# A third W' buffer, loads at set steps, low words on GpSimd and new priorities in a planned attention-and-FFN kernel

## Chip, cores and metric

The kernel runs on one core of one Trainium2 chip. The metric is the time of one execution on the device in microseconds (us). The core has five engines that matter here: TensorE (PE in the profile, with its weight loads as PEld), VectorE (DVE), ScalarE (ACT), GpSimd (POOL) and SyncE (SP), which starts all the DMA transfers. Each of them works through its own instructions in the order in which the program holds them.

## The reference

Eight batches of eight heads, 576 rows of 64 numbers each. Thirty-two packed queries per head first attend over keys and values; then every query attends over the 32 packed results. A feed-forward layer with GELU follows, whose weights arrive as 64-bit floats.

```python
def sm_attn(qq, kk, vv):
    s = scale * np.matmul(qq, kk.transpose(0, 1, 3, 2))
    a = np.exp(s - np.max(s, axis=-1, keepdims=True))
    a = a / (np.sum(a, axis=-1, keepdims=True) + 1e-09)
    return np.matmul(a, vv)
p_packed = sm_attn(p, k, v)            # 8 x 8 x 32 x 64
x = sm_attn(q, p_packed, p_packed)     # then as 4608 x 512
h = x @ w_in                           # 512 x 2048
g = 0.5 * h * (1.0 + erf(h * inv_sqrt2))
out = g @ w_out                        # 2048 x 512
```

## The kernel before

**Tiling.** Batches go in four pairs (NP), the 2048 hidden units in four blocks of 512 (NF), so there are 16 units u (NU), each with eight steps: j is the batch of the pair, c one of four groups of 128 hidden units. A step n is a *hidden product* (h, L1184: twelve products of a three-part split, or L1175 in unit 0, plain 32-bit), a GELU on ScalarE (L1206), a split of its result into two words (L1213 on ScalarE, L1215 on VectorE, GpSimd for the rest of the rows in L1226 and L1227) and an *output product* (o, three times four products in L1236 to L1238), with one more set for the edge rows in each unit (o_edge).

**W'.** The second attention's product with the packed results and the first layer are folded: W' = packed results times w_in (`packed_w_in`, L1118, tile wps). It runs on the array in 64x32 tiles, where the others use it whole. ScalarE rounds it (L1129) and VectorE takes the rest (L1134). One buffer for each j, `wps[0]` and `wps[1]`, holds the result; it comes free with the last hidden product of its j. Both its PSUM tile and those of hidden products and of most scores come from `wide`, which has two.

**Weights.** They are decoded from 64-bit to two 32-bit words: ScalarE takes the absolute value of the high word (L1052) and scales the low word (L1053), VectorE repairs the exponent (L1060, L1061) and puts the sign in (L1066), GpSimd adds (L1080, L1088) and, for w_out, subtracts (L1094). The first pass stores them (`ws`); pairs 1 to 3 read them back (w<-ws, L1017).

**Attention.** For each chunk of four heads: transposes of keys and queries, key scores (L657), exponential (L739), transposes of it (L761, L764) and their copies (L771, L774), packed products (L799), query scores, centring (L878), exponential (L884), scaling (L898). In pair 0, keys and queries are loaded in rows of whole heads (L553) and transposed by TensorE with copies by ScalarE or VectorE (L592, L596); `FIRST` says which engine does what. In later pairs they are loaded in four blocks for each half (L563) and transposed by VectorE (L581). A pair's attention runs beside the hidden and output products of the pair ahead of it.

**Order.** All of it is written out while the program is built. Each piece of work is a task; it yields an `Op` with an engine and an assumed duration, or an `Event` that it waits for. `Order` plays the tasks through once to find how long the chain behind each is, corrects that by the tables SLACK, EARLY and SOONER, and plays them again: a free engine takes the ready Op of the highest priority whose buffers are free (`issue`), and its instructions are written in that order. So the tables set every engine's order, SyncE's too. On the chip an engine waits at an instruction whose input is late, and all behind it wait too. Before the first output product, a free TensorE gets a dummy product (L1157). `LATER["from"]` says at which step of the block ahead a pair's work may begin (`pair_started`); all its loads may then go.

A tile whose buffer was first lent to a dummy carries the name "idle" in the profile; only L1157 is a dummy.

Of the kernel before, what the change touches and what calls it, by code (L numbers as in the profile page):

```python
# [19 lines left out]
P = 128  # L20
# [26 lines left out]
MODE_SWITCH = 0.1  # L47
# [5 lines left out]
    "batch0": 1.805,  # L53
    "batch1": 2.067,
    "attention": 2.371,
    "load0": 0.169,
    "load": 0.137,
    "w_in0": 3.068,
    "w_out0": 1.984,
    "w_in": 0.766,  # L60
    "w_out": 1.189,
    "packed_w_in": 1.103,
# [3 lines left out]
    "batch0": 14.5,  # L66
    "batch1": -9.1,
    "attention": -0.5,
    "load0": -0.0,
    "load": 9.1,  # L70
    "w_in0": 3.4,
    "w_out0": 7.3,
    "w_in": -0.4,
    "w_out": -4.9,
    "packed_w_in": -4.5,
    "steps": -3.6,
# [3 lines left out]
    "0_0_0": 13.7,  # L80
    "0_0_1": 16.8,
    "0_1_0": -11.6,
    "0_1_1": -4.7,
    "0_2_0": -3.1,
    "0_3_0": -1.5,
    "0_4_0": -28.2,
    "0_5_0": -0.7,
    "chunk_0_0": -19.0,
    "chunk_0_1": 89.8,
    "chunk_1_0": -3.5,  # L90
    "chunk_1_1": -5.4,
    "softmax1": 48.6,
    "softmax1_0_0": 40.2,
    "softmax1_0_1": 36.3,
    "softmax1_1_0": -5.1,
    "softmax1_1_1": -10.6,
    "softmax2": -48.0,
    "softmax2_0_0": -26.1,
    "softmax2_0_1": -48.7,
    "softmax2_1_0": -69.0,  # L100
    "softmax2_1_1": -47.5,
    "wp_0_0": -28.4,
    "wp_0_1": 17.6,
    "wp_1_0": -21.6,
    "wp_1_1": -51.8,
# [21 lines left out]
    "from": (2, 0, 0, 0),  # L127
# [33 lines left out]
    "turn": {"k": ('ACT', 'ACT', 'ACT', 'ACT'), "q": ('ACT', 'DVE', 'ACT', 'ACT')},  # L161
# [21 lines left out]
class Ring:  # L183
# [7 lines left out]
    def has_room(self, name, before=0):  # L191

        if self.order.dry:
            return True
        n = len(self.held) + before
        if self.names and self.names[n] != name:
            return False
        return n < self.bufs or self.held[n - self.bufs] is None
# [64 lines left out]
class Order:  # L263
# [105 lines left out]

    def issue(self, engine):  # L370
        ready = self.ready[engine]
        for i, (_, _, op, go_on, begin) in enumerate(ready):
            if not op.takes or all(r.has_room(name, n if r is op.takes[0][0] else 0) for n, (r, name) in enumerate(op.takes)):
                del ready[i]
                break
# [55 lines left out]
def packed_attention_gelu_ffn(ctx: ExitStack, tc: tile.TileContext, q, k, v, p, w_in, w_out, out):  # L431
# [27 lines left out]
    def plan(order):  # L459
# [5 lines left out]

        def small(i, b):
# [18 lines left out]
        wraws = ring("wraw", 2, [P, FB, 2], I32)  # L485
# [3 lines left out]
        wps = [ring(f"wp{j}", 1, [P, 2, 2, FB], F32R) for j in range(2)]  # L489
# [9 lines left out]
        wps[0].names = ["q_0_1"] + [f"wp_{u}_0" for u in range(NU)]  # L499
        wps[1].names = ["v_0_1"] + [f"wp_{u}_1" for u in range(NU)]  # L500
# [20 lines left out]
        a2_used, plain_a2_ready = ([Event(n) for _ in range(2)] for n in (1, 2))  # L521
        pair_started = [Event() for _ in range(NP + 1)]
        scored = [Event(4) for _ in range(NP)]
        a2T, plain_a2, pp = {}, {}, {}
# [24 lines left out]

        def load(bt, name, src, c, step):  # L550
# [14 lines left out]
            cost, fn = ((1, 590e3), rows) if bt.b < 2 else ((4, 1640e3, 2), blocks)  # L565
# [41 lines left out]
        def load_values(s, step):  # L607
            heads = slice(4 * s.hh, 4 * s.hh + 4)

            def fn(t):  # L610
# [3 lines left out]
                nc.sync.dma_start(tail, v[s.b, heads, 512:S].rearrange("g p d -> p g d"))  # L614

            s.v = yield Op(DMA, (2, 830e3), step, fn, [(s.v_ring, f"v_{s.n}")])
            fire(s.v_loaded)

        def packed_queries(bt, step):
# [4 lines left out]

            raw = yield Op(DMA, (2, 225e3), step, fetch, [(praws, f"p_{bt.n}")])
# [34 lines left out]
        def scores_of_batch(bt, name, which, lhs, evacuate, engine, cost, step):  # L660
            xTs = [bt.xT[name, c].rearrange("p (g x) -> p g x", g=2) for c in range(2)]

            def part(half):
                cols = slice(half * HALF, (half + 1) * HALF)
                t = yield Op(
                    PE, 0.68, step,
# [20 lines left out]
        def rows_in_order(t):  # L687

            return t.rearrange("p (x t e) -> p e t x", t=NT, e=2)

# [3 lines left out]
        def scores1_of_chunk(s, step):  # L694
            yield from transposed(s.bt, "k", s.hh, step)
            yield s.bt.p_ready
            xT = of_heads(s.bt.xT["k", s.hh])
            s.t1 = yield Op(
                PE, 0.68, step,
# [27 lines left out]
        def softmax1(ss, step):  # L727
# [6 lines left out]
            def exps():  # L734
                for s in ss:
                    src, dst = s.e1, s.e1
                    if s.b < 2:
                        src, dst = s.t1[:, :, :HALF].rearrange("p e (t x) -> p e t x", t=NT), rows_in_order(s.e1)
# [3 lines left out]
                ACT, (1.22 if ss[0].b < 2 else 0.76) * n, step, exps, table="exp", hold=held("softmax1", ss[0]))  # L742
# [11 lines left out]
        def packed(s, step):  # L754
# [3 lines left out]

            def most(t):
                for i in range(4):  # L760
                    nc.tensor.transpose(bank(t)[:, i * P:(i + 1) * P], s.e1[:, i:512:4], ident)  # L761

            def least(t):
                nc.tensor.transpose(t[:64, :P], s.e1[:, 512:S], ident)  # L764
# [8 lines left out]
            def copy_least(t):  # L773
                nc.scalar.copy(e1T[:64, 4], t[:64, :P])  # L774
# [10 lines left out]
            if ring_ is wide:  # L785
                yield from piece("e1Tm", 0.52, both, 0.63, copy_both)
            else:
                yield [piece("e1Tm", 0.48, most, 0.48, copy_most), piece("e1Tn", 0.11, least, 0.16, copy_least)]
# [12 lines left out]
            t = yield Op(PE, 0.85, step + 1, product, [(ring_, f"pp_{s.n}")], busy=False)  # L801
# [19 lines left out]
        def scores2_of_chunk(s, step):  # L821
# [4 lines left out]
                PE, 0.68, step,  # L826
# [61 lines left out]
        def weights2(s, step):  # L888
# [10 lines left out]
            if s.b < 2:  # L899
# [4 lines left out]
                fire(plain_a2_ready[s.b])  # L904
# [86 lines left out]
        def plain(u):  # L991

            return u == 0
# [417 lines left out]
```

## Time and profile before

| what | value |
|---|---|
| median of 3 runs | 738.14 us (737.36 to 738.2) |
| the profiled execution | 735.98 us |
| its span, first to last instruction | 734.2 us |
| granted TensorE clock | 1.000 |
| HBM read, written | 83.89 MB, 22.02 MB |
| SyncE's k loads, each | 48 of 144.0 KB, 5.0 us to landing |
| SyncE's w reloads, each | 72 of 512.0 KB, 5.0 us to landing |

The profile has one row for each group of instructions: line, engine, operation, output<-inputs by the program's names, shape, count, then busy time in us, the mean of one in ns, and the idle time of the engine ahead of them with what ended it. Matmuls overlap one another, so the step from the start of one to the start of the next says what one costs. A busy TensorE may be busy with dummies.

### The profile page before, as it was taken

Reading aid. Unit: us, or ns where it says so; the run is one execution under the profiler, and the core shown is the slowest. Engines: PE = TensorE matmul, PEld = TensorE weight load, DVE = VectorE, ACT = ScalarE, POOL = GpSimd, SP = SyncE. Lnnn points to the kernel's source line nnn. Section 1 sums busy time; section 2 is a strip of 40 time slices with the busy share of each in tenths; the row PEclk is TensorE's granted clock in tenths of the full one; section 3 lists DMA queues with packets and bytes.
Section 4 is the critical chain, followed back from the end, with each engine's and each line's share of the span. In section 5 each row is a group of like instructions: output and inputs, shape, how many; then the busy total and the mean of one; then the engine's idle time right before and its main releaser. Section 6 shows DMA issues by size and latency. Waiting matters only on the chain.

```text
span 734.2 us, 13174 instructions
## 1 busy us (share of the span) xinstructions
PE 720.6 (98%) x5263; PEld 580.7 (79%) x5263; DVE 388.5 (53%) x611; ACT 357.1 (49%) x604; POOL 151.9 (21%) x312
## 2 busy tenths in 40 slices
PE   8999998999999998999999999999999999999998
PEld 6777785887778787788877878788777888888886
DVE  5899756988683323732767231553558321333332
ACT  6897746856653332544444443354455343333231
POOL 2544644644311110010110101111011101111010
PEclk9999999999999999999999999999999999999999
DMA  8949998666527995242243999222241702213021
GB/s 306 372 184 183 283 236 221 190 194 216 173 59 226 147 170 178 34 171 67 65 167 127 208 162 217 40 98 78 62 173 58 244 1 85 89 38 106 8 108 71
DMA packets 156588, 106.76 MB, mean 145 GB/s; under 512 B 124272, under 2 KB 132464, under 8 KB 156528
## 3 DMA queue, kind: packets, MB, share of 16 engines
q1 hardware_dynamic: 156528, 105.93, 55.4%
q8 instruction: 41, 0.67, 0.4%
q14 instruction: 19, 0.16, 0.1%
HBM read 83.89 MB, written 22.02 MB: 144 GB/s over the span
## 4 chain that ended last, share of the span: by engine, by line
PE 82%; DMA 7%; SPq 3%; ACT 3%; DVE 3%; issue 1%; DVEq 0%; ACTq 0%
PE h L1184 23%; PE o L1236 14%; PE o L1238 14%; PE o L1237 13%; PE wps L1118 4%; DMA wraw<-in_moe_w_in_dram 4%; SPq L563 3%; PE h L1175 2%; PE o_edge L1236 2%; PE o_edge L1238 2%; PE o_edge L1237 2%; PE pp L799 2%; DMA wraw<-in_moe_w_out_dram 1%; PE s L657 1%; DMA k<-in_k_dram 1%
## 5 line engine op out<-in xcount | busy, mean ns | idle before, releaser
L1184 PEld LDWEIGHTS h<-a2T,wp 128*128 128x128 f32 x1440 | 202.1, 188 | 22.3 <-issue 4.2
L1184 PE MATMUL h<-a2T,wp 128*128 128x288 f32 x1440 | 211.6, 296 | 3.4 <-ACT e L717 1.6
L1236 PE MATMUL o<-w,g 128*128 128x512 f32 x508 | 205.1, 404 | 2.3 <-DMA w<-ws 2.3
L1238 PE MATMUL o<-w,g 128*128 128x512 f32 x508 | 199.1, 392 | 1.9 <-DVE g L1215 1.9
L1206 ACT ACTIVATE graw<-h 128x576 f32<-128x576 f32 x128 | 83.4, 652 | 241.0 <-PE h L1184 219.1
L1237 PE MATMUL o<-w,g 128*128 128x512 f32 x508 | 198.5, 391 | 0.0
L1215 DVE TENSOR_TENSOR g<-graw,g 128x512 fp32r<-128x512 f32 x128 | 95.1, 743 | 181.8 <-ACT g L1213 181.3
L1226 POOL CAST t<-graw 128x64 fp32r<-128x64 f32 x128 | 37.2, 291 | 500.1 <-ACT graw L1206 393.4
L1236 PEld LDWEIGHTS o<-w,g 128*128 128x128 f32 x508 | 95.4, 188 | 40.3 <-issue 22.5
L1238 PEld LDWEIGHTS o<-w,g 128*128 128x128 f32 x508 | 95.4, 188 | 24.9 <-DVE g L1215 3.8
L1237 PEld LDWEIGHTS o<-w,g 128*128 128x128 f32 x508 | 95.5, 188 | 14.8
L1213 ACT CAST g<-graw 128x512 fp32r<-128x512 f32 x128 | 79.5, 621 | 3.3
L1322 DVE TENSOR_TENSOR acc<-o,acc 128x512 f32<-128x512 f32 x96 | 63.1, 683 | 30.3 <-PE o L1238 30.3
L1134 DVE TENSOR_TENSOR wp<-wps,wp 128x1024 fp32r<-128x1024 f32 x30 | 36.5, 1218 | 51.2 <-ACT wp L1129 51.1
L1129 ACT CAST wp<-wps 128x1024 fp32r<-128x1024 f32 x30 | 30.4, 1014 | 54.6 <-PE wps L1118 54.6
L1227 POOL TENSOR_TENSOR t<-graw,t 128x64 fp32r<-128x64 f32 x128 | 46.5, 363 | 10.2
L1118 PE MATMUL wps<-w,pp 64*32 64x512 f32 (+1 forms) x544 | 35.4, 575 | 0.0
L1052 ACT ACTIVATE wt<-wraw 128x512 f32<-128x512 f32 x32 | 21.6, 674 | 23.1 <-DMA wraw<-in_moe_w_in_dram 14.7
L581 DVE STREAM_TRANSPOSE kT<-k 128x1152 f32<-128x1152 f32 x12 | 16.5, 1376 | 26.4 <-DMA k<-in_k_dram 26.3
L1088 POOL TENSOR_TENSOR wt<-wt 128x512 int32<-128x512 int32 x16 | 21.9, 1367 | 28.0 <-DVE wt L1066 20.7
L1080 POOL TENSOR_TENSOR w<-wt 128x512 int32<-128x512 int32 x16 | 21.0, 1314 | 23.7 <-DVE wt L1066 9.2
L1060 DVE TENSOR_SCALAR wt<-wt 128x512 f32<-128x512 f32 x32 | 17.2, 538 | 15.5 <-ACT wt L1052 15.5
(120 smaller groups left out, 667.8 us busy)
## 6 DMA issues: line engine op xcount, KB each, us to landing
w<-ws SPq DMA_DIRECT2D x72, 512.0 KB, 5.0
ws<-w SPq DMA_DIRECT2D x24, 512.0 KB, 5.4
wraw<-in_moe_w_in_dram SPq DMA_DIRECT2D x16, 512.0 KB, 5.0
wraw<-in_moe_w_out_dram SPq DMA_DIRECT2D x16, 512.0 KB, 6.1
v<-in_v_dram SPq DMA_DIRECT2D x16, 512.0 KB, 6.5
k<-in_k_dram SPq DMA_DIRECT2D x48, 144.0 KB, 5.0
q<-in_q_dram SPq DMA_DIRECT2D x48, 144.0 KB, 4.7
out_dram<-acc SPq DMA_DIRECT2D x27, 256.0 KB, 2.1
```

The source lines that it names most:

```text
L1118: nc.tensor.matmul(t[r0:r0 + 32, hh, :m], lhsT=pp[b][rows, hh, r0:r0 + 32], rhs=wi[u, hh][rows, g, cols], start=True, stop=True)
L1134: yield Op(DVE, 1.2, step, lambda: nc.vector.tensor_tensor(lo, x, hi.bitcast(F32), ALU.subtract))
L1184: nc.tensor.matmul(t[:, half, :HALF], lhsT=w[:, wpart, ch, fc], rhs=a2T[b, ch][:, apart, half * HALF:(half + 1) * HALF], start=ch == 0 and ...
L1206: lambda raw: nc.scalar.activation(raw.rearrange("p (a n) -> p a n", a=2), t[:, :, :HALF], AF.Gelu),
L1213: g = yield Op(ACT, 0.52, lead, lambda g: nc.scalar.copy(g[:, 0], main), [(gts, f"g_{n}")])
L1215: DVE, 0.6, lead, lambda: nc.vector.tensor_tensor(g[:, 1], main, g[:, 0].bitcast(F32), ALU.subtract),
L1226: nc.gpsimd.tensor_copy(dst[:, 0], side)
L1227: nc.gpsimd.tensor_tensor(dst[:, 1], side, dst[:, 0].bitcast(F32), ALU.subtract)
L1236: nc.tensor.matmul(t, lhsT=g[0], rhs=w[:, 0], start=first, stop=False)
L1237: nc.tensor.matmul(t, lhsT=g[0], rhs=w[:, 1], start=False, stop=False)
L1238: nc.tensor.matmul(t, lhsT=g[1], rhs=w[:, 0], start=False, stop=last)
L1322: yield Op(DVE, 0.6, n, lambda: nc.vector.tensor_tensor(a, x, a, ALU.add))
```

## The change

Six things change, and all priorities with them.

1. *Third W' buffer.* `wps` has three buffers. Up to unit 3 each j has its own, as before; from unit 4 on the products take the three in turn. Until the last weight is decoded, the third is split in two and holds raw weights, in place of a ring of its own (`Parts`, `undecoded`).
2. *Choice on TensorE.* Once outputs run (`steady`), `next_on_pe` chooses: while the array is used whole, a lone tiled product is passed over until a second is ready or it has waited 9.5 us; while it is tiled, a tiled product goes first.
3. *Loads at set steps.* A later pair's loads each wait for their own step of the block ahead (`begun`, `at_step`, `LATER["at"]`), and keys, queries and values go in a fixed order (`LATER["order"]`, `names`). `LATER["from"]` changes from (2, 0, 0, 0) to (0, 5, 8, 0).
4. *Key scores in another column order* in pair 0: the product reads the keys in the order in which their scores are kept later, and the exponential writes its row contiguously where it wrote it scattered. The last transposes and their copies become two of 32 rows each, and the last value rows come by two DMAs in place of one.
5. *Engines in pair 0 and unit 0.* GpSimd scales six of the eight low words, and centres and scales three chunks in place of one. VectorE copies two of four W' products, and the keys of one chunk; ScalarE copied these.
6. *Assumed durations and tables* are fitted anew. Their values are left out below but for three lines.

```diff
-MODE_SWITCH = 0.1
+MODE_SWITCH = 0.115
+PATIENCE = 9.5
...
 EARLY = {
-    "batch0": 14.5,
-    "batch1": -9.1,
...
+    "batch0": 49.2,
+    "batch1": 2.3,
...
-    "from": (2, 0, 0, 0),
+    "from": (0, 5, 8, 0),
+    "order": "k00 k01 k10 q00 q01 k11 q10 q11",
+    "at": {"p": (2, 10), "k": (0, 0, 5, 1), "v": (3, 4, 0, 5), "q": (2, 5, 9, 12)},
...
-    "gpsimd": (1,),
-    "copy": ('ACT', 'ACT', 'ACT', 'ACT'),
-    "banks": (True, False, False, True),
-    "small": (True, True, True, True),
+    "gpsimd": (0, 1, 2),
+    "plain": 2,
+    "low": (True, True, False, True, True, True, True, False),
+    "copy": ('ACT', 'DVE', 'ACT', 'DVE'),
+    "banks": (False, True, False, False),
+    "small": (False, True, True, True),
...
-    "turn": {"k": ('ACT', 'ACT', 'ACT', 'ACT'), "q": ('ACT', 'DVE', 'ACT', 'ACT')},
+    "turn": {"k": ('ACT', 'DVE', 'ACT', 'ACT'), "q": ('ACT', 'DVE', 'ACT', 'ACT')},
...
+class Parts:
+    def __init__(self, whole):
+        self.whole, self.n = whole, 0
+    def tile(self, *args, **kwargs):
+        self.n += 1
+        t = self.whole[:, self.n % 2].rearrange("p a b -> p (a b)").bitcast(I32)
+        return t.rearrange("p (n t) -> p n t", t=2)
...
+    def next_on_pe(self, ready):
+        first = tiled = other = None
+        for i, (_, _, op, _, begin) in enumerate(ready):
+            if not self.issuable(op):
+                continue
+            if first is None:
+                first = i
+                if not op.cost or op.busy and self.whole:
+                    return i
+                late = self.now >= begin + PATIENCE
+            if op.cost and not op.busy:
+                if tiled is not None or not self.whole or late:
+                    return i if tiled is None else tiled
+                tiled = i
+            elif other is None:
+                other = i
+        return first if other is None else other
...
+        def wp_ring(u, j):
+            return wps[j] if u < NF else wps[(2 * (u - NF) + j + 2) % 3]
...
-        wraws = ring("wraw", 2, [P, FB, 2], I32)
-        wps = [ring(f"wp{j}", 1, [P, 2, 2, FB], F32R) for j in range(2)]
+        wps = [ring(f"wp{j}", 1, [P, 2, 2, FB], F32R) for j in range(3)]
+        home = wps[2].take("wraws")
+        wraws = Ring(order, Parts(home), None, 2, None, None)
+        undecoded = Event(4 + 8 * (NF - 1))
+        undecoded.waiting.append(lambda: wps[2].give(home))
...
+        def at_step(b, name, i):
+            if b >= 2:
+                yield begun[(b // 2 - 1) * STEPS + LATER["at"][name][i]]
...
-            xT = of_heads(s.bt.xT["k", s.hh])
+            xT = s.bt.xT["k", s.hh].rearrange("p (t h x) -> p h x t", t=NT, h=4)
...
-                        src, dst = s.t1[:, :, :HALF].rearrange("p e (t x) -> p e t x", t=NT), rows_in_order(s.e1)
+                        src, dst = s.t1[:, :, :HALF], s.e1.rearrange("p (e c) -> p e c", e=2)
...
             def least(t):
-                nc.tensor.transpose(t[:64, :P], s.e1[:, 512:S], ident)
+                if s.b >= 2:
+                    nc.tensor.transpose(t[:64, :P], s.e1[:, 512:S], ident)
+                    return
+                for e in range(2):
+                    nc.tensor.transpose(t[:32, e * P:e * P + P], s.e1[:, e * HALF + 256:e * HALF + HALF], ident)
...
+            on_pool = u == 0 and FIRST["low"][2 * i + part if i < 2 else 2 + i]
             def both_words(both):
                 nc.scalar.activation(both[:, 0].bitcast(F32), high.bitcast(F32), AF.Abs)
-                nc.scalar.activation(both[:, 1], low.bitcast(U32), AF.Copy, scale=2.0 ** -29)
+                if not on_pool:
+                    nc.scalar.activation(both[:, 1], low.bitcast(U32), AF.Copy, scale=2.0 ** -29)
+            def low_word():
+                yield Op(
+                    POOL, 1.0, step,
+                    lambda: nc.gpsimd.tensor_scalar(both[:, 1], low.bitcast(U32), 2.0 ** -29, None, ALU.mult))
```

More of the change, by code (lines that the diff above doesn't have):

```diff
@@ L52 @@
 SLACK = {
[L53 to L62, printed above, removed]
+    "batch0": 2.516,
+    "batch1": 2.386,
+    "attention": 1.933,
+    "load0": 0.141,
+    "load": 0.371,
+    "w_in0": 4.854,
+    "w_out0": 2.339,
+    "w_in": 0.143,
+    "w_out": 1.903,
+    "packed_w_in": 1.985,
     "steps": 0.535,
@@ L65 @@
 EARLY = {
-    "batch0": 14.5,
-    "batch1": -9.1,
[L68 to L76, printed above, removed]
+    "batch0": 49.2,
+    "batch1": 2.3,
+    "attention": -0.2,
+    "load0": -5.3,
+    "load": 9.2,
+    "w_in0": -7.6,
+    "w_out0": 8.8,
+    "w_in": 0.2,
+    "w_out": -13.2,
+    "packed_w_in": -2.4,
+    "steps": -2.7,
 }
 SOONER = {
[L80 to L105, printed above, removed]
+    "0_0_0": 3.9,
+    "0_0_1": 44.4,
+    "0_1_0": 2.9,
+    "0_2_0": -8.3,
+    "0_3_0": -1.9,
+    "0_4_0": -30.3,
+    "0_5_0": -2.6,
+    "chunk_0_0": -31.8,
+    "chunk_0_1": 61.1,
+    "chunk_1_0": -6.5,
+    "chunk_1_1": -11.3,
+    "softmax1": 167.0,
+    "softmax1_0_0": 4.6,
+    "softmax1_0_1": -11.7,
+    "softmax1_1_0": 99.0,
+    "softmax1_1_1": -147.5,
+    "softmax2": 14.7,
+    "softmax2_0_0": 101.1,
+    "softmax2_0_1": -218.4,
+    "softmax2_1_0": -290.2,
+    "softmax2_1_1": -163.2,
+    "wp_0_0": -175.4,
+    "wp_0_1": -99.0,
+    "wp_1_0": 52.5,
+    "wp_1_1": -196.8,
 }
@@ L195, in has_room @@
         n = len(self.held) + before
-        if self.names and self.names[n] != name:
+        if self.names and self.names[n] not in (None, name):
             return False
@@ L368, in clock, with issuable @@
         return need
+    def issuable(self, op):
+        return all(r.has_room(name, n if r is op.takes[0][0] else 0) for n, (r, name) in enumerate(op.takes))
+    def next_on_pe(self, ready):
[15 more added lines that the diff above has]
+        return first if other is None else other
     def issue(self, engine):
         ready = self.ready[engine]
[L372 to L375, printed above, removed]
+        best = None
+        if engine == PE and self.steady:
+            best = self.next_on_pe(ready)
+        else:
+            for i, entry in enumerate(ready):
+                if self.issuable(entry[2]):
+                    best = i
+                    break
+        if best is not None:
+            _, _, op, go_on, begin = ready.pop(best)
         else:
@@ L563, in blocks @@
                         nc.sync.dma_start(t[32 * i:32 * i + 32], view[j])
[L565 removed]
+            yield from at_step(bt.b, name, 2 * bt.j + c)
+            cost, fn = ((1, 590e3), rows) if bt.b < 2 else ((4, 1800e3, 2), blocks)
             bt.raw[name, c] = yield Op(
@@ L1120, in product @@
                                 rhs=wi[u, hh][rows, g, cols], start=True, stop=True)
-            t = yield Op(PE, 0.16 + 0.87 * m / FB, step, product, [(wide, f"wps_{u}_{j}_{part}")], busy=False)
+            t = yield Op(PE, 0.05 + 0.9 * m / FB, step, product, [(wide, f"wps_{u}_{j}_{part}")], busy=False)
             for i in range(2):
```

106 lines of the change are left out of this document (66 added, 40 removed).

## The prediction

> **What bounds the kernel now.** I read the page first: is one engine full, and from when to when?
>
> ```profile
> span 734.2 us, 13174 instructions
> PE 720.6 (98%) x5263; PEld 580.7 (79%) x5263; DVE 388.5 (53%) x611; ACT 357.1 (49%) x604; POOL 151.9 (21%) x312
> ...
> L1157 PE MATMUL idle<-still 128*128 128x256 bf16 x151 | 21.0, 287 | 1.1 <-DVE still L455 1.1
> ```
>
> TensorE is busy 98% of the span, but 21.0 us of that is line 1157, the dummy product that keeps its clock up while it has nothing to do. A change that leaves the useful products as they are can win only in four places: dummies, true idle time, changes between full and tiled use of the array, and the tail. So the second view is a table of busy time by stage, first for all engines, then for line 1157 alone (the columns are the stretch, its length, busy time and count for PE, PEld, DVE, ACT, POOL, then the granted clock, the DMA share and GB/s):
>
> ```profile
> 10.00:24.00 14.00, 14.00 (x218) 10.60 (x217) 9.38 (x22) 11.60 (x26) 5.09 (x4) 1.00 1.07 357
> 24.00:41.80 17.80, 17.75 (x283) 13.23 (x281) 15.23 (x34) 15.76 (x37) 8.06 (x6) 1.00 1.00 368
> ...
> 48.00:84.00 36.00, 36.00 (x180) 27.51 (x179) 31.95 (x43) 28.74 (x47) 18.69 (x25) 1.00 1.02 199
> 84.00:724.00 640.00, 632.31 (x4456) 514.51 (x4455) 318.16 (x494) 291.45 (x483) 114.46 (x268) 1.00 0.51 130
> 724.00:734.20 10.20, 6.55 (x29) 5.08 (x28) 3.91 (x6) 0.00 (x0) 0.00 (x0) 1.00 0.35 129
> ...
> 10.00:48.00 38.00, 14.44 (x109) 10.30 (x109) 1.00 0.91 319
> ```
>
> From 10 to 48 us, 14.4 us of TensorE are dummies: **the first pair's attention** is not TensorE's problem; ScalarE (15.76 of 17.80), VectorE (15.23) and DMA (share 1.00) are all nearly full. From 48 to 84 TensorE lacks nothing. From 84 to 724 it is idle for 640.00 - 632.31 = 7.7 us. The tail of 3.65 us is not touched. The granted clock is 1.00 throughout, so there is nothing to win or lose there.
>
> Third view, the waits of TensorE from 80 us on, those over 1 us (what waited, for whom, us in total, times, the longest):
>
> ```profile
> PE o L1236 <- DMA w<-ws: 2.3, 1, 2.3
> PE o L1238 <- DVE g L1215: 1.9, 3, 1.2
> PE h L1184 <- ACT e L717: 1.6, 1, 1.6
> ```
>
> These three are one story, loads of a later pair in the way, which the queues show:
>
> ```profile
> 234.26 21.09 SPq L563 DMA_DIRECT2D k<-in_k_dram  x16
> 259.37 13.91 SPq L563 DMA_DIRECT2D q<-in_q_dram  x12
> 273.37 4.75 SPq L1017 DMA_DIRECT2D w<-ws  x6
> ...
> 245.27 1.38 DVE L581 STREAM_TRANSPOSE kT<-k 128x1152 f32<-128x1152 f32 x1 [6.24 <-DMA k<-in_k_dram]
> 246.57 0.65 DVE L1215 TENSOR_TENSOR g<-graw,g 128x512 fp32r<-128x512 f32 x1
> ...
> 117.27 0.66 ACT L1052 ACTIVATE wt<-wraw 128x512 f32<-128x512 f32 x1 [2.39 <-DMA wraw<-in_moe_w_in_dram]
> ```
>
> As soon as a pair may start, SyncE issues all its key loads, 16 for 21 us, then the queries. The reload of weights is issued behind them at 273.37, and the output product waits 2.3 us for it. VectorE stands in its fixed order at a key transpose (L581) for 6.24 us, with the L1215 behind it that the output needs. ScalarE stands in the same way at a weight load before it can empty key scores (L717).
>
> **The change, part by part.**
>
> *Loads at set steps.* No load is removed. For each pair they are released over the steps 0 to 12 of the block before instead of together, and the tables order keys and queries. The three waits above, 5.8 us, all come from loads in a bunch; I take 4.5 us off, leaving 1.3 for one bunch that stays (the first three key loads are still released at step 5 or before, and these loads together keep their transfer time). Bounds: 0, if the bunch only moves, and 7.7, all idle time of that stretch. The steps are new waits: nothing is queued behind them in SyncE's order, since that order is fixed when the program is written, but a key that comes late blocks VectorE at L581 with the L1215 behind it, as at 245 us.
>
> *Tiled products side by side.* What does a change of the array's use cost?
>
> ```profile
> 600.81 0.39 PE L1237 MATMUL o<-w,g 128*128 128x512 f32 x1
> 601.04 0.39 PE L1238 MATMUL o<-w,g 128*128 128x512 f32 x1
> 601.36 1.09 PE L1118 MATMUL wps<-w,pp 64*32 64x512 f32 x16
> 602.38 0.50 PE L1236 MATMUL o<-w,g 128*128 128x512 f32 x1
> 602.71 0.39 PE L1237 MATMUL o<-w,g 128*128 128x512 f32 x1
> ```
>
> Output matmuls start 0.23 us apart (600.81 to 601.04); before the tiled group the step is 0.32, after it 0.33 (602.38 to 602.71). So each tiled group costs 0.09 + 0.10, about 0.2 us. In TensorE's order from 84 us on I count 45 such groups, of which these are the first and the last:
>
> ```profile
> 96.85 1.09 PE L1118 MATMUL wps<-w,pp 64*32 64x512 f32 x16
> ...
> 702.88 1.09 PE L1118 MATMUL wps<-w,pp 64*32 64x512 f32 x16
> ```
>
> That is 9 us in all: 29 products of W' (L1118), the scores (L657) and the packed products (L799), some merged already. The third buffer lets both W' products of a block stand ready together from the fifth block on: 24 products in 12 groups, of which 2 are merged today: 10 groups fewer. The new choice of TensorE's next product, which passes a lone tiled product over until a second is ready, may merge some five more of scores and packed products. 15 x 0.2 = 3.0 us; bounds 0 and 25 x 0.2 = 5.0.
>
> *The buffer's other use.* It holds the raw weights until the last is decoded. ScalarE's busy time in the low words (L1053) from 214 us on, where the fifth block's first W' product stands:
>
> ```profile
> 214.00:734.20 520.20, 0.00 (x0) 1.00 0.46 113
> ```
>
> None is left by then. Nothing counted; if the decoding ran late, that product would wait.
>
> *The first pair.* Rows for one instruction (busy, mean ns):
>
> ```profile
> L739 ACT ACTIVATE e<-idle,mx 128x576 f32<-128x576 f32 x2 | 2.8, 1392 | 0.0
> L739 ACT ACTIVATE e<-e,mx 128x576 f32<-128x576 f32 x12 | 9.2, 766 | 0.0
> L1053 ACT ACTIVATE wt<-wraw 128x512 int32<-128x512 uint32 x32 | 21.4, 669 | 0.0
> L1129 ACT COPY wp<-wps 128x512 f32<-128x512 f32 x4 | 2.3, 583 | 0.6 <-PE wps L1118 0.6
> L774 ACT COPY e1T<-e1Tn 64x128 f32<-64x128 f32 x4 | 1.1, 265 | 0.0
> L878 DVE TENSOR_TENSOR e<-e,mx 128x576 f32<-128x576 f32 x15 | 12.5, 847 | 0.0
> L878 POOL TENSOR_TENSOR e<-e,mx 128x576 f32<-128x576 f32 x1 | 1.5, 1535 | 3.2 <-DVE mx L853 3.2
> L1080 POOL TENSOR_TENSOR w<-wt 128x512 int32<-128x512 int32 x16 | 21.0, 1314 | 23.7 <-DVE wt L1066 9.2 <-ACT wp L1129 4.8 <-ACT e L717 4.8
> ```
>
> ScalarE loses: four exponentials that no longer write a scattered row, at 1.39 - 0.77 each, 2.5 us; six low words, 6 x 0.67 = 4.0; two W' copies, 2 x 0.58 = 1.2; one chunk's three key copies, about 3 x 0.45 = 1.3 (384 of L1129's 512 columns). It gains four small copies, 4 x 0.27 = 1.1. Net -7.9 us. VectorE gets those two W' and three key copies (some 2.5 us, if as long as on ScalarE) and gives two chunks' centring and scaling, 4 x 0.85 = 3.4, to GpSimd: 0.9 us less. GpSimd gets 4 x 1.5 = 6.0 and six low words, which no row shows: between the 0.67 of ScalarE and 1.31 of L1080, the same size on the same engine, which I take: 7.9. Together +13.9 us on an engine that has room (8.06 of 17.80). The key scores read their moving operand with a wider step: nothing, or at worst twice the time of four groups, each 1.09 x 288/512 = 0.6 us by L1118's row: +2.4. Value loads get one DMA more each, four issues, under the other transfers; if that cover is gone, they take SyncE 4 x 1.2 us (13.91 / 12 above), 4.6 us.
>
> Not all 7.9 us stand on the path: three resources are full, the loads among them, and the same bytes must come. And GpSimd's work reaches into VectorE's:
>
> ```profile
> 6.53 0.43 DVE L1060 TENSOR_SCALAR wt<-wt 128x512 f32<-128x512 f32 x1 [1.16 <-ACT wt L1052]
> ...
> 8.35 1.52 DVE L1060 TENSOR_SCALAR wt<-wt 128x512 f32<-128x512 f32 x1 [0.20 <-ACT wt L1052]
> ...
> 8.30 1.28 POOL L1080 TENSOR_TENSOR w<-wt 128x512 int32<-128x512 int32 x1 [7.00 <-DVE wt L1066]
> ```
>
> The same instruction takes 0.43 us alone and 1.52 when it begins beside a GpSimd product: 1.1 us more. The Trainium skill (SBUF — State Buffer, section SBUF: two separate sides) gives the reason: the two share a port pair that the first holds for its whole instruction, while the other fully blocks. By that rule the ten new GpSimd instructions could cost VectorE their whole 13.9 us; the rows agree with its kind, and the sum goes by them. At 1.1 us for each of ten, VectorE loses up to 11 us between 6 and 48, where it is idle only 2.6 us of the 17.8 up to 41.8. So I take 2.5 us off, a third of ScalarE's relief; bounds: -7.9 (all of it), +6 (11 us of blocking less half that falls into pauses).
>
> *Refitted priorities* reorder all of this; no row prices them, and they are inside these bounds. For waits that the new order opens I add 1.5 us, about one wait of the 1.6 us kind above.
>
> Sum: -4.5 - 3.0 - 2.5 + 1.5 = -8.5 us. The profiled execution took 735.98 us (span 734.2 and 1.8 around it), 2.2 below the median of 738.14; taken off the median: **729.6 us**, 1.2% faster.
>
> **The rivals.**
>
> *The first pair shrinks more.* ScalarE's whole relief reaches the end (14.4 us of dummies leave room for it), and no new wait opens. Then -4.5 - 3.0 - 7.9 = -15.4: about 722.7. For it: ScalarE at 89% from 24 to 41.8. Against it: DMA share 1.00 up to 41.8.
>
> *It does not do what it says.* Pairs do not form, since a tile of PSUM must be free for each (two such tiles serve the hidden, W' and score products), and the loads collide elsewhere: only half of the stalls go, -2.5: about 735.6, still faster by 0.3%. At zero it would be no change.
>
> *Slower: a pair holds both wide tiles.* While both W' products stand there, no hidden product can begin.
>
> ```profile
> L1129 ACT CAST wp<-wps 128x1024 fp32r<-128x1024 f32 x30 | 30.4, 1014 | 54.6 <-PE wps L1118 54.6
> L1134 DVE TENSOR_TENSOR wp<-wps,wp 128x1024 fp32r<-128x1024 f32 x30 | 36.5, 1218 | 51.2 <-ACT wp L1129 51.1
> ```
>
> The first tile is free 1.0 + 1.0 + 1.2 and some 0.4 us of handing over after the pair's begin, 3.6 us. TensorE has the second product, 1.0, and output matmuls: with the twelve of a step (12 x 0.23 = 2.7) it is covered, 3.7. With six there is a stall of 1.2 us; 12 pairs, 14.4 us: 744.0. It decides from the point where fewer than some eleven output matmuls lie between a pair and the next hidden product. For it: the 1.6 us wait for L717, the same kind. Against it: outputs trail the hidden products by a step, and L1134 waits for nothing but L1129. The Trainium skill says as much (TensorEngine Tiling, section PSUM Bottleneck): tiling speeds up TensorE but not the emptying of PSUM. Lone W' products of today lose nothing to it in this trace; no row shows a pair.
>
> **How the numbers follow.** My forecast has 0.54 (725 to 734), the first pair's large gain 0.15 (718 to 725), little or no effect 0.13 (734 to 739), slower 0.18. A measurement of this kernel can tell about 0.2%, 1.5 us, from no change. Of the third case, 0.06 lies within that. Faster 0.76, same 0.06, slower 0.18. Range 718 to 742: below it lies only all three gains at their bounds, -7.7 - 5.0 - 7.9 = -20.6 or 717.5; above it the stall in more than ten of the twelve pairs (729.6 + 10 x 1.2 = 741.6). That leaves out 0.03 and some 0.14.
>
> **What would show it.** Loads: no w<-ws wait of 2 us and no DVE wait of 6 us at L581. Pairs: tiled groups after 84 us at about 30 instead of 45, L1118's successors 32 matmuls long. First pair: the first hidden product, now here,
>
> ```profile
> 41.84 2.21 PE L1175 MATMUL h<-a,wp 128*128 128x288 f32 x8
> ```
>
> 2 to 3 us sooner, dummies from 10 to 48 nearer 12 than 14.4, the exponential at 0.77. Wrong, if hidden products wait for the W' tile's emptying, if L1060 or L1215 in the first 48 us grow by more than the relief, or if the idle time from 84 us on stays at 7.7 us.

## The result, and the profile after

The changed kernel takes **727.59 us** (median of 4 runs, 727.48 to 728.0) where the kernel before took 737.75 in the same comparison: ratio 0.9871, 95% interval 0.9845 to 0.9898. The forecast was 729.6, range 718 to 742. The sum came out; its terms did not, and one had the wrong sign. Of 54 executions of the kernel before in the comparisons below, the nine with a mean granted clock of 0.995 took 740.3 us in the median and the 21 with 0.999 or more 736.1, so the 10.2 us between the medians hold some lost clock; the two profiled executions, both at 1.00, differ by 8.4 us and their spans by 8.7.

The page, and the dummy's row from the groups by line:

```profile
span 725.5 us, 13221 instructions
PE 718.1 (99%) x5274; PEld 585.0 (81%) x5274; DVE 390.3 (54%) x612; ACT 352.5 (49%) x597; POOL 166.1 (23%) x322
...
L1252 PE MATMUL idle<-still 128*128 128x256 bf16 x158 | 22.1, 287 | 1.0 <-DVE still L499 1.0
```

There are not fewer dummies but 1.1 us more. The table by stage (columns as before; the last row is the dummy line alone):

```profile
24.00:41.80 17.80, 17.80 (x313) 12.63 (x310) 13.27 (x30) 14.83 (x36) 10.01 (x8) 1.00 0.93 336
48.00:84.00 36.00, 36.00 (x198) 27.23 (x196) 29.26 (x47) 28.32 (x44) 19.80 (x25) 1.00 1.02 223
84.00:715.30 631.30, 629.50 (x4455) 520.06 (x4454) 324.31 (x495) 293.78 (x488) 118.33 (x271) 1.00 0.52 132
715.30:725.50 10.20, 6.46 (x29) 5.02 (x27) 3.81 (x6) 0.00 (x0) 0.00 (x0) 0.97 0.35 129
...
10.00:48.00 38.00, 12.98 (x94) 8.70 (x94) 1.00 0.88 305
```

ScalarE and VectorE are less busy from 24 to 41.8 us, as forecast, but the first hidden product came at 44.78 us and not sooner than the 41.84 of the kernel before. The idle time of TensorE from 84 us on is 631.30 - 629.50 = 1.8 us where it was 7.7; the tail is the same. TensorE's waits from 40 us on, all of them:

```profile
PE h L1279 <- ACT e L782: 0.7, 2, 0.4
PE o_edge L1331 <- DVE wp L1229: 0.7, 1, 0.7
PE h L1279 <- ACT graw L1301: 0.2, 1, 0.2
```

None for a load is left. Two tables worked out from TensorE's order say where the 8.7 us of span come from. In the first, each kind of product is counted from its start to the next start, the last output up to the end of the span:

| us of TensorE | before | after | |
|---|---|---|---|
| shown as idle | 8.6 | 2.4 | -6.1 |
| dummies | 18.8 | 19.7 | +0.8 |
| output products with edges | 412.3 | 407.6 | -4.7 |
| hidden products | 207.6 | 206.8 | -0.9 |
| W' | 32.8 | 31.4 | -1.4 |
| scores, both kinds | 19.2 | 22.3 | +3.1 |
| packed products, transposes | 33.9 | 34.3 | +0.5 |

The number of output products is the same, so the 4.7 us of the outputs are changes of array use and waits too short for the view of idle time. The 3.1 us of the scores had no place in the sum, which took nothing for them. The second table has the end of output step n (us from the span's start; the experiments stand below):

| n | before | after | old read | half dummies | choice by priority | two buffers | other value |
|---|---|---|---|---|---|---|---|
| 1 | 50.8 | 54.3 | 51.3 | 50.4 | 54.3 | 54.5 | 54.3 |
| 8 | 83.8 | 89.0 | 86.0 | 85.1 | 89.4 | 89.2 | 89.0 |
| 32 | 222.2 | 222.3 | 219.3 | 218.3 | 225.1 | 222.4 | 226.4 |
| 64 | 398.3 | 392.7 | 389.8 | 388.5 | 399.0 | 395.1 | 398.0 |
| 128 | 727.7 | 718.9 | 716.0 | 714.7 | 725.5 | 724.2 | 724.4 |

The first pair comes out **3.5 us later**; units 1 to 3 win that back (from +5.2 to 0), and units 4 on win 8.9.

### The profile page after: what moved, and what is told of

It reads as the page before. It is cut to its first block, busy times and chain, and to the rows that moved or that the text cites. A ratio compares the mean times of both kernels' runs of the same rounds, so it can differ in the third digit from the quotient of the medians.

```text
span 725.5 us, 13221 instructions
## 1 busy us (share of the span) xinstructions
PE 718.1 (99%) x5274; PEld 585.0 (81%) x5274; DVE 390.3 (54%) x612; ACT 352.5 (49%) x597; POOL 166.1 (23%) x322
## 4 chain that ended last, share of the span: by engine, by line
PE 97%; DMA 1%; ACT 1%; SPq 0%; DVE 0%; issue 0%; ACTq 0%
PE h L1279 27%; PE o L1331 17%; PE o L1333 16%; PE o L1332 16%; PE wps L1213 4%; PE s L726 3%; PE h L1270 2%; PE o_edge L1331 2%; PE o_edge L1333 2%; PE o_edge L1332 2%; PE idle L1252 2%; PE pp L877 2%; DMA k<-in_k_dram 1%; PE e1Tm L831 1%; PE qm L653 1%; PE km L653 0%
## 5 line engine op out<-in xcount | busy, mean ns | idle before, releaser
L1331 PEld LDWEIGHTS o<-w,g 128*128 128x128 f32 x508 | 95.4, 188 | 32.8 <-issue 15.7
L1322 POOL TENSOR_TENSOR t<-graw,t 128x64 fp32r<-128x64 f32 x128 | 46.1, 360 | 10.2
L1213 PE MATMUL wps<-w,pp 64*32 64x512 f32 (+1 forms) x528 | 32.4, 576 | 0.0
L1331 PE MATMUL o_edge<-w,t 128*128 128x512 f32 x64 | 25.1, 393 | 0.7 <-DVE wp L1229 0.7
L1175 POOL TENSOR_TENSOR w<-wt 128x512 int32<-128x512 int32 x16 | 22.6, 1412 | 13.1 <-DVE wt L1154 11.0
L1332 PE MATMUL o_edge<-w,t 128*128 128x512 f32 x64 | 25.0, 390 | 0.0
L1333 PE MATMUL o_edge<-w,t 128*128 128x512 f32 x64 | 25.0, 390 | 0.0
```

The costliest lines, as they stand in the source:

```text
L1213: nc.tensor.matmul(t[r0:r0 + 32, hh, :m], lhsT=pp[b][rows, hh, r0:r0 + 32], rhs=wi[u, hh][rows, g, cols], start=True, stop=True)
L1322: nc.gpsimd.tensor_tensor(dst[:, 1], side, dst[:, 0].bitcast(F32), ALU.subtract)
L1331: nc.tensor.matmul(t, lhsT=g[0], rhs=w[:, 0], start=first, stop=False)
L1332: nc.tensor.matmul(t, lhsT=g[0], rhs=w[:, 1], start=False, stop=False)
L1333: nc.tensor.matmul(t, lhsT=g[1], rhs=w[:, 0], start=False, stop=last)
```

## The experiments

### The wide key read

Only two views change, in the order of the changed kernel:

```diff
-xT = s.bt.xT["k", s.hh].rearrange("p (t h x) -> p h x t", t=NT, h=4)
+xT = of_heads(s.bt.xT["k", s.hh])
...
-src, dst = s.t1[:, :, :HALF], s.e1.rearrange("p (e c) -> p e c", e=2)
+src, dst = s.t1[:, :, :HALF].rearrange("p e (t x) -> p e x t", t=NT), s.e1.rearrange("p (e x t) -> p e x t", e=2, t=NT)
```

> The changed kernel with one line pair turned round: the key scores of the first pair read the keys with x innermost again (contiguous runs of 32), and the exponential reads PSUM in the wide step and still writes contiguously. The order of all instructions on all engines is that of the changed kernel. Theory (the wide step of TensorE's moving operand costs 0.72 us in each of four score products, and it stands on the path to the first hidden product, which came 2.9 us later than in the kernel before): the products go from 1.37 to 0.65 us, the first hidden product comes 2 to 3 us sooner than 44.8, and the time falls by 2 to 3 us, to about 725. Rival (GpSimd's centring and scaling of the first two chunks, 1.2 to 1.4 us each, sets the first hidden product): the products get shorter, the first hidden product moves by less than 1 us and the time by less than 1 us. If the exponential is dear when it reads PSUM in a wide step, it shows as more than 0.74 us.

Measured 725.42 us (ratio to the kernel before 0.9818, 0.9792 to 0.9845), 2.2 below the changed kernel. TensorE in order of time, the changed kernel first: a key score group, its next start, the first hidden product, the first output product under its own name.

```profile
12.62 1.45 PE L726 MATMUL s<-kT,pT 64*32 64x288 f32 x16
14.00 0.72 PE L1252 MATMUL idle<-still 128*128 128x256 bf16 x5
...
44.78 2.21 PE L1270 MATMUL h<-a,wp 128*128 128x288 f32 x8
...
52.24 0.39 PE L1331 MATMUL o<-w,g 128*128 128x512 f32 x1
```

The experiment:

```profile
12.46 0.72 PE L726 MATMUL s<-kT,pT 64*32 64x288 f32 x16
13.11 0.72 PE L1252 MATMUL idle<-still 128*128 128x256 bf16 x5
...
41.78 2.21 PE L1270 MATMUL h<-a,wp 128*128 128x288 f32 x8
...
49.23 0.39 PE L1331 MATMUL o<-w,g 128*128 128x512 f32 x1
...
L804 ACT ACTIVATE e<-s,mx 128x576 f32<-128x576 f32 x4 | 2.9, 737 | 3.0 <-DVE mx L797 3.0
```

A group costs 0.65 us instead of 1.38, four of them 2.9, and the first hidden product comes 3.0 us sooner, where the kernel before had it (41.84). The span is 2.9 us shorter, the median 2.2. The exponential still takes 0.74, so ScalarE's gain is had without the wide read. The theory held: the key read stands on the path. TensorE shows no wait from 12 us up to there; it works through products and a fixed number of dummies.

### What a new order costs by itself

Any edit that changes the plan gives an order for which the tables were not fitted. Two controls on the changed kernel and one on the kernel before show what that alone does.

```diff
-    "batch1": 2.386,
+    "batch1": 2.45,
```

> The changed kernel with one table value moved by 3% (SLACK batch1 2.386 to 2.45), which gives another order on all engines from the first pair on, and nothing else. It shows what loss of fit alone costs in the other runs. Theory (the edits carry the gain): within 2 us of 727.6. Rival (the gain is the fit of the tables): 4 us or more slower.

Measured 734.73 us (0.995, 0.9929 to 0.9971), 7.1 above the changed kernel, as the rival had it. The first output step ended at 57.9 us, 3.6 later; 3.5 more were lost afterwards.

```diff
-    "attention": -0.2,
+    "attention": 0.3,
```

> The changed kernel with another table value moved (EARLY attention -0.2 to 0.3): the order is that of the changed kernel through the first pair and differs from about unit 1 or 2 on. It shows how much of the loss of the first run of this kind (7 us, half of it in the first 55 us) belongs to later units. Theory: 0 to 2 us slower. Rival (every order that the tables were not fitted for loses some 4 us in the later units as well): 3 us or more slower.

Measured 732.88 (0.9949, 0.9929 to 0.9969), 5.3 above, the rival again, and all of it after step 26 (last column of the table). The same step in the kernel before:

```diff
-    "attention": -0.5,
+    "attention": 0.0,
```

> The kernel before with the table value moved that was moved in the changed kernel (EARLY attention, by 0.5). The order stays that of the kernel before up to about unit 1. The changed kernel lost 5 us by it. Theory (the kernel before was fitted as closely): 3 to 6 us slower than the kernel before. Rival (the refit is a gain of its own, and the kernel before did not stand at such a point): within 2 us.

Measured 742.48 against 737.5 (ratio 1.007, 1.0045 to 1.0096): 5.0 us slower, as the theory had it and as in the changed kernel. So in these three tries a table moved by a little cost 5 to 7 us, in either kernel. An undone part that is planned anew must be read from the kind of loss in its trace, not from its time alone. The row by stage up to the tail and a stretch of 3.4 us, first in the second control, then in the kernel before with its value moved:

```profile
84.00:720.90 636.90, 631.64 (x4455) 520.68 (x4454) 327.88 (x495) 293.10 (x488) 118.42 (x271) 1.00 0.50 130
328.90:332.30 3.40, 3.40 (x22) 1.31 (x21) 2.23 (x3) 2.12 (x4) 0.56 (x2) 0.51 0.00 0
...
84.00:730.70 646.70, 637.61 (x4464) 518.70 (x4463) 324.09 (x495) 293.09 (x485) 115.28 (x269) 0.99 0.51 130
253.70:257.10 3.40, 3.40 (x10) 2.66 (x9) 1.71 (x2) 0.00 (x0) 0.00 (x0) 0.50 1.48 142
```

Lost fit shows in two ways. One is idle time: 636.90 - 631.64 = 5.3 us in the second control, against 1.8 in the changed kernel. The other is lost clock: 1.4 us behind its longest wait (1.9 us), the granted clock is 0.51 for 3.4 us. By these two numbers I estimate 1.7 us of longer products. Together that is nearly the whole loss, with 40 tiled groups (stretches of tiled products without a whole-array product between) as in the changed kernel. The first control has one such stretch of low clock too, from 150.5 us. In the kernel before, the moved value adds only 1.4 us of idle time (9.1 against 7.7); two stretches of low clock, from 175.2 and 253.7, are about 3.4 us more by the same estimate. The rest is changes of array use: 50 tiled groups where it had 45.

### TensorE's choice, and the third buffer

```diff
-        if engine == PE and self.steady:
-            best = self.next_on_pe(ready)
-        else:
-            for i, entry in enumerate(ready):
+        for i, entry in enumerate(ready):
```

> The changed kernel with TensorE's next product chosen by priority alone, as before; the third buffer and all else stay. Theory (the choice saves changes of array use at 0.2 us each): tiled groups after 84 us rise from 40 to 50 or more, the time rises by 2 to 3 us, to about 730. Rival (pairs would form by priority anyway and the choice mostly delays tiled products): groups stay near 40 and the time within 1 us, or lower.

Measured 734.33 us (0.9938, 0.9915 to 0.9961), 6.7 above the changed kernel, more than the 2 to 3 of the theory, with 54 tiled groups after 84 us where that has 40 and the kernel before had 45. Its row:

```profile
84.00:721.90 637.90, 635.28 (x4467) 517.88 (x4468) 323.47 (x496) 293.01 (x488) 118.35 (x271) 1.00 0.52 131
```

Idle is 2.6 us, only 0.8 more than in the changed kernel, the granted clock has no low stretch before the tail, and the first step ends at the same time. So this loss has not the kind of the two controls on the changed kernel: it lies in busy time at full clock. What a merge saves is seen at a pair in the changed kernel:

```profile
244.53 0.40 PE L1333 MATMUL o<-w,g 128*128 128x512 f32 x1
244.85 1.95 PE L1213 MATMUL wps<-w,pp 64*32 64x512 f32 x32
246.73 0.50 PE L1331 MATMUL o<-w,g 128*128 128x512 f32 x1
247.06 0.39 PE L1332 MATMUL o<-w,g 128*128 128x512 f32 x1
```

Two products take 246.73 - 244.85 = 1.88 us, where two alone took 1.02 each, and only one change of array use is paid, 0.19: a pair costs 2.07 against 2.42, **0.35 saved**. Fourteen groups more are 4.9, if each costs as much as at this pair; with 0.8 of idle that is 5.7 of the 6.7, and the last 1.0 wasn't traced to a line. A new order alone can move this number too: it added five groups to the kernel before and took two from the changed kernel (38 in the first control). So most of the fourteen, but not surely all, belong to the choice.

The third buffer, undone:

```diff
-            return wps[j] if u < NF else wps[(2 * (u - NF) + j + 2) % 3]
+            return wps[j]
```

> The changed kernel with W' kept in one buffer for each j in all units: the third buffer only holds raw weights and is then unused. Theory (the third buffer lets two W' products stand side by side): no two W' products follow each other from unit 4 on, tiled groups after 84 us rise from 40 to 46 or more, the time rises by 2 to 4 us. Rival (the choice of TensorE's next product pairs them with scores and packed products as well): groups stay below 44 and the time within 1.5 us.

Measured 732.52 us (0.9946, 0.9924 to 0.9967), 4.9 above. From unit 4 on no two W' products touch, where the changed kernel has six such pairs; but the choice joins W' with scores or packed products, eight times in place of six, and the groups are only 43, as the rival had it; its time, within 1.5 us, it missed. Three groups are 1.1 us. Of the rest, these waits from 215 us on are 3.2, in place of 0.7:

```profile
PE h L1279 <- ACT graw L1301: 1.8, 2, 1.3
PE pTm L698 <- ACT graw L1301: 0.8, 1, 0.8
PE ppTm L891 <- ACT graw L1301: 0.6, 1, 0.6
```

They are of the controls' kind. So the choice still finds partners without the third buffer. What that buffer adds may be the 1.1 us; but an order alone moved the groups by two in the first control, so that even this can't be told from lost fit with certainty, and the remainder not at all.

### The loads

All loads together, steps and fixed order taken out:

```diff
-    "from": (0, 5, 8, 0),
+    "from": (2, 0, 0, 0),
...
         def at_step(b, name, i):
-            if b >= 2:
-                yield begun[(b // 2 - 1) * STEPS + LATER["at"][name][i]]
+            return
+            yield
```

> The changed kernel without set steps: a later pair's loads may all go when the pair begins, the pairs begin at steps 2, 0, 0, 0 as before, and no order of loads is fixed; priorities as in the changed kernel. Theory (the loads in a bunch made 8 us of waits, shown and hidden): VectorE waits 5 us or more again for keys at the key transposes, TensorE's idle time after 84 us goes from 1.8 back to 5 to 9 us, the time rises by 4 to 8 us, to 732 to 736. Rival (the refitted tables did it): the time rises by no more than in the run with one table value changed, and no wait for loads comes back.

Measured 736.28 (0.997, 0.995 to 0.999), 8.7 above. But where is it lost?

```profile
84.00:214.00 130.00, 123.28 (x953) 98.34 (x951) 94.96 (x147) 81.41 (x142) 59.05 (x76) 0.99 0.75 213
214.00:723.80 509.80, 508.09 (x3527) 420.89 (x3526) 228.74 (x351) 214.12 (x347) 59.66 (x196) 1.00 0.46 113
```

6.7 us of idle lie before 214 us, where pair 1's loads meet the decoding (1.05 in the changed kernel), and 1.7 behind it; a stretch of low clock, 0.50 from 133.4 us, costs about 1.7 more by the estimate above. So the idle time of 5 to 9 us that the theory named is back, but hardly where the bunch was: from 215 us on VectorE waits 12.3 us for keys (6.3 in the changed kernel), yet TensorE only 0.7 for w<-ws. Before 214 us it also is a new order, and the longest wait there, 2.1 us ahead of a W' product, has no releaser in the view, so the loads' share stays open. Two sharper edits leave everything up to about 230 us in place: steps and order for pairs 2 and 3 alone put into the kernel before, and taken from the changed kernel.

```diff
 in the kernel before:
+        def at_step(b, name, i):
+            if b >= 4:
+                yield begun[(b // 2 - 1) * STEPS + LATER["at"][name][i]]
...
-    "from": (2, 0, 0, 0),
+    "from": (2, 5, 8, 0),
```

> The kernel before with one part of the change: the loads of pairs 2 and 3 wait for their set steps and go in the fixed order; pair 1's loads and all tables stay. The order of all engines is that of the kernel before up to about 230 us. Theory (bunched loads made the waits between 245 and 280 us and at 422 us, 4.1 us shown as idle and about 0.6 hidden in longer steps): these waits go and the time falls by 4 to 5 us against the kernel before. Rival (a new order without fitted tables gives it back elsewhere, as the run with one table value did): within 1 us of the kernel before or slower, with new waits after 230 us.

Measured 736.29 against 736.44 (0.9986, 0.9967 to 1.0005): no difference that shows, as the rival had it. VectorE's wait for keys from 230 us on, first in the kernel before, then here, and TensorE's waits here:

```profile
DVE kT L581 <- DMA k<-in_k_dram: 24.6, 8, 6.2
...
DVE kT L592 <- DMA k<-in_k_dram: 0.5, 1, 0.5
...
PE h L1197 <- ACT graw L1219: 1.4, 2, 0.8
PE o_edge L1249 <- ACT graw L1219: 1.2, 1, 1.2
PE h L1197 <- DVE e L861: 0.4, 2, 0.2
```

In the kernel before, TensorE waited 4.2 us there for w<-ws and g. The mechanism is right: set steps take these waits away. But 2.6 us of others open, behind GELU, and the groups go from 45 to 47. The trace of this run lay 1.9 us behind that of the kernel before at the end of step 32, ahead of the edit's reach, and 0.7 behind at the end, so the trace alone speaks for at most 1.2 us. The other way round:

```diff
 in the changed kernel:
-            if b >= 2:
+            if 2 <= b < 4:
...
-    "from": (0, 5, 8, 0),
+    "from": (0, 0, 0, 0),
```

> The changed kernel with the loads of pairs 2 and 3 let go together when the pair begins (steps 0, 0 of the block ahead), without the fixed order for them; pair 1 keeps its set steps, so that the order is that of the changed kernel up to about unit 3. Theory (set steps keep the bunch from the output products): waits for w<-ws or behind key transposes come back between 215 and 440 us, the time rises by 3 to 5 us. Rival (the longer transfer time that the planner now assumes, and its margins, suffice): less than 1 us.

Measured 728.43 us (0.9893, 0.987 to 0.9915), 0.8 above the changed kernel, as the rival had it.

```profile
PE o L1331 <- DMA w<-ws: 0.6, 1, 0.6
```

That is the one wait of TensorE that returns. So in the changed kernel the steps of pairs 2 and 3 are worth about 1 us; whether the longer transfer times that the planner now assumes, or the new priorities, keep the other old waits away wasn't tried.

### The dummies, and GpSimd's share

On the kernel of the first experiment, in its order:

```diff
-                    nc.tensor.matmul(bank(t)[:, :256], lhsT=still[:, :P], rhs=still, start=True, stop=True)
+                    idles.append(order.now)
+                    if order.now < 10 or len(idles) % 2:
+                        nc.tensor.matmul(bank(t)[:, :256], lhsT=still[:, :P], rhs=still, start=True, stop=True)
```

> The first experiment's kernel (old key read, order of the changed kernel) without every second dummy product after 10 us of the plan, some 50 of 0.11 us each, 5.5 us of TensorE. All other instructions and their order stay. Theory (in the first 52 us TensorE never waits: its dummies, counted out by the plan, and its own products set the pace, which is why ScalarE's relief of 7.9 us did not show): the first output product comes 2 to 5 us sooner than 49.2 and the time falls by 2 to 4 us, to about 722. Rival (the dummies only cover waits for ScalarE, VectorE, GpSimd and the loads): TensorE waits instead, the first output product moves by less than 1 us, the time stays within 1 us; lower granted clock or longer products would make it slower.

Measured **723.3 us** (0.9807, 0.9779 to 0.9835), the shortest of the kernels that do the whole work. The first hidden and the first output product:

```profile
41.10 2.21 PE L1274 MATMUL h<-a,wp 128*128 128x288 f32 x8 [0.81 <-DVE a L980]
...
48.30 0.40 PE L1335 MATMUL o<-w,g 128*128 128x512 f32 x1
```

The first output comes 0.9 us sooner, not 2 to 5; now TensorE waits for VectorE. So the dummies hid about 1 us that was to be had, and the data set the rest: neither expectation came out as a whole. The span is 1.2 shorter (721.4 against 722.6), the median 2.1.

Then none of them from 10 us of the plan on:

```diff
-                    if order.now < 10 or len(idles) % 2:
+                    if order.now < 10:
```

> The same without any dummy after 10 us of the plan, some 100. Theory: sooner still than with half of them, by 1 to 3 us, until the data set the pace. Rival (TensorE's clock needs them): products in the first 50 us take up to twice their time, and the time is above 725.

Measured 723.52 (0.9813, 0.9781 to 0.9845): nothing more, where the theory had 1 to 3 us. The granted clock drops from 10 to 24 us:

```profile
10.00:24.00 14.00, 10.83 (x170) 7.61 (x170) 11.38 (x25) 8.76 (x21) 9.36 (x7) 0.88 1.07 356
```

With half of the dummies it is 1.00 there. The drop is one stretch, 0.50 for 3.4 us from 16.2 us on. The rival's fear came true in small, and the time stayed.

With half of the dummies again, GpSimd's low words are replaced by zeros, and its subtractions and products in the second softmax are cut to one of 18 blocks of 32 columns. The kernel leaves this part of the computation out:

```diff
-                    lambda: on(engine).tensor_tensor(u, u, per_block(m[:, 0, s.i, :NB32]), ALU.subtract), port=True)
+                    lambda: on(engine).tensor_tensor(*[x[:, :1] if engine == POOL else x for x in (u, u, per_block(m[:, 0, s.i, :NB32]))], ALU.subtract), port=True)
...
-            yield Op(engine, cost, step, lambda: on(engine).tensor_tensor(u, u, per_block(r), ALU.mult), port=True)
+            yield Op(engine, cost, step, lambda: on(engine).tensor_tensor(*[x[:, :1] if engine == POOL else x for x in (u, u, per_block(r))], ALU.mult), port=True)
...
-                    lambda: nc.gpsimd.tensor_scalar(both[:, 1], low.bitcast(U32), 2.0 ** -29, None, ALU.mult))
+                    lambda: nc.gpsimd.memset(both[:, 1], 0))
```

> As the run with half of the dummies, but GpSimd's share in the first pair is cut: it fills the low words of six weights of the first unit with zeros in place of scaling them, and centres and scales one of 18 blocks of 32 columns in its three chunks. So part of the computation is left out. Theory (GpSimd's added 14 us are beside the path): the first output product and the time stay within 1 us of the run with half of the dummies. Rival (GpSimd's slower steps and its hold on VectorE's port set the first pair): 2 us or more sooner.

Measured 722.24 us (0.9792, 0.9764 to 0.9821), 1.1 below the run with half of the dummies; the first output product starts here, 1.2 sooner:

```profile
47.12 0.39 PE L1335 MATMUL o<-w,g 128*128 128x512 f32 x1
```

That lies between the two expectations: cutting these instructions from 17.0 to 5.0 us of GpSimd frees about 1 us. In the changed kernel, two low words (L1140), each with the VectorE row that begins beside it, and the second VectorE instruction of the decoding in the first 48 us, before and after, show what they touch:

```profile
5.82 1.53 POOL L1140 TENSOR_SCALAR wt<-wraw 128x512 int32<-128x512 uint32 x1 [4.53 <-DMA wraw<-in_moe_w_in_dram]
...
6.46 0.43 DVE L1147 TENSOR_SCALAR wt<-wt 128x512 f32<-128x512 f32 x1 [1.37 <-ACT wt L1133]
...
12.35 1.64 POOL L1140 TENSOR_SCALAR wt<-wraw 128x512 int32<-128x512 uint32 x1
...
L1140 POOL TENSOR_SCALAR wt<-wraw 128x512 int32<-128x512 uint32 x3 | 4.8, 1598 | 4.7 <-DMA wraw<-in_moe_w_in_dram 4.5
...
13.47 0.79 DVE L1147 TENSOR_SCALAR wt<-wt 128x512 f32<-128x512 f32 x1
...
L1061 DVE TENSOR_SCALAR wt<-wt 128x512 int32<-128x512 int32 x8 | 3.4, 427 | 0.3
...
L1148 DVE TENSOR_SCALAR wt<-wt 128x512 int32<-128x512 int32 x8 | 6.6, 821 | 0.3
```

A low word takes 1.5 to 1.6 us, above my upper bound of 1.31. L1147 took 0.79 us beside one low word and 0.43 beside the other, so not every meeting costs. Over the first 48 us VectorE's three decoding instructions (L1060, L1061, L1066; after L1147, L1148, L1154) take 17.2 us where they took 14.8, 2.4 more and not up to 11.

## Why the prediction was right, point by point

**The sum** of -8.5 came to -10.2 by the medians and -8.7 by the spans. It came right by luck, through two errors that cancelled. The first pair is 6.0 us worse than forecast (+3.5 in place of -2.5). From the end of output step 1 to that of step 128 the change wins 12.3 us (676.9 to 664.6), where the other three terms add up to -6.0. Of these 12.3, waits that the view shows are 5.9 and five tiled groups about 1.8; the rest lies in many small steps, and no run says which part of the change brings it.

**Loads, -4.5.** Right about which waits go: the three, 5.8 us, are gone, and 0.7 us of the third's kind (h<-e) stands at two other places. Wrong about their price as a part: for pairs 2 and 3 by themselves, the set steps gave nothing that shows in the kernel before and are worth 0.8 us in the changed one. Where waits were taken away, waits behind GELU opened, 2.6 us of them; the 1.5 us that I had set aside for the whole change were too few for an order without fit. For pair 1's loads the size stays open.

**Side by side, -3.0.** The mechanism was right, the size of a merge was not: 0.35 us, as the array is also quicker within a pair (0.94 for a product, not 1.02), where I took 0.2 from the edges alone. I expected 30 groups and there are 40, with six pairs of W' and not twelve. Five groups fewer than before are 1.8 us. But with the choice taken out, the plan has 54 groups, and the kernel loses 6.7 us. That is the largest loss from one edit that isn't of the controls' kind, though some of the groups may come from the new order.

**The first pair, -2.5.** This step failed, +3.5 at the first output. Its failing term is the key read, which I valued at nothing with +2.4 as the worst: it is 2.9 us, all on the path. One read lies 128 32-bit numbers behind the other, and a group took 1.38 us against 0.65 with runs of 32. The Trainium skill (Advanced Engine Details and Errata, section SBUF Cachelines) asks for at least two hits on a 16-byte line for full speed. The trace agrees, since at this step there is one hit on a line. Of the other 3 us of the miss, 2.5 are the part of ScalarE's relief that I put on the path: of its 7.9 us none reached the first output, for with the old read it starts at 49.2 us, before at 48.7. Dummies hide about 1 us of it and GpSimd's slower steps take about 1: with the old read, half of the dummies and GpSimd's share cut, the first output starts at 47.12, 1.6 us sooner than before. What sets the rest wasn't tested; with half of the dummies TensorE waits for VectorE's transposes (a, L980).

**Refitted priorities, within bounds.** They were the largest unknown. In three tries a small move of one value cost 5 to 7 us, most of the forecast's whole gain. But the kernel before lost as much by the same move (5.0 us), so that it isn't shown that the refit as such gained anything. I had also written that the clock of 1.00 leaves nothing to win or lose: in the controls each stretch of low clock cost about 1.7 us, by the estimate above.

**The rivals.** That a pair holds both wide tiles and stops the hidden products did not happen: all waits after 40 us are 1.6 us together. That the first pair shrinks more was wrong: it grew. That no pairs form was wrong: six of W' did from unit 4 on.

## What to carry to other kernels

In a kernel whose order is planned and fitted, undo a part with the order kept, or read the kind of the loss (idle time, lost clock, changes of array use, longer products) beside a control that changes the order alone. Here ScalarE did the reading in wide steps at no cost that shows, where TensorE took 2.9 us for it: same output, 2.2 us less by the medians. Work taken from an engine that looked full won nothing at the first output here, while TensorE's own queue, its dummies included, set the pace up to it.

## What was not expected of the hardware

ScalarE read PSUM in steps of 128 bytes as fast as contiguously (0.74 us for 128x576 in both), though it took 1.33 to 1.39 to write SBUF scattered. TensorE's moving operand at a step of 512 bytes took 2.1 times as long. GpSimd took 1.5 to 1.6 us for a one-input scaling of 512 columns, more than for a sum of two inputs (1.3 us). Without dummies the granted clock was 0.88 from 10 to 24 us, and the time was the same, 723.5 against 723.3. In four other runs the granted clock fell to half for 3.4 us ahead of the tail (five times in all), each time 0.4 to 1.4 us behind a wait of 1.4 to 2.1 us; the kernel before had a wait of 2.3 us at 276.9 without such a fall.
